# Decode attention with gated feed-forward: scores moved to TensorE, values to VectorE, larger tiles in one ring

## The chip, the cores and the metric

The kernel runs on one core of a Trainium2 chip. A core has a matrix engine (TensorE, PE in the profile, with its weight loads PEld), a vector engine (VectorE, DVE), a scalar engine (ScalarE, ACT), GpSimd (POOL) and SyncE (SP), whose queue issues the transfers here. Each engine takes its own instructions in order and waits on semaphores for the others. Sixteen DMA engines move data from the main memory (HBM) into the on-chip memory (SBUF, 128 partitions); TensorE writes its results to PSUM. The metric is the device time of one execution in microseconds (us), the median of several runs.

## What is computed

For two sequences of one token each, the output is `g * attention + (1 - g) * feed_forward`, all in float32:

```python
B, Sq, D = 2, 1, 448
H, Sk, Dh = 16, 4096, 256          # Dff = 1792

q = (x @ wq).reshape(B, Sq, H, Dh).transpose(0, 2, 1, 3)
scores = jnp.einsum("bhqd,bhkd->bhqk", q, k_cache) * (Dh ** -0.5)
p = softmax(scores)
o = jnp.einsum("bhqk,bhkd->bhqd", p, v_cache)
a = o.transpose(0, 2, 1, 3).reshape(B, Sq, H * Dh) @ wo

b = relu(x @ w1) @ w2
g = sigmoid((x * gate_w).sum(-1, keepdims=True))
return g * a + (1 - g) * b
```

Keys and values are 32 units (16 heads, 2 sequences) of 4096 x 256 numbers each, 4 MB a unit and cache, 268.4 MB together. The weights are another 21.1 MB. Each number is used once.

## The kernel before

A unit `u` is one head `h` and one sequence `b`. Its 4096 keys come as two tiles `k_sb` of 2 MB (128 partitions, 16 keys of 256 numbers in each, a row of 16,384 bytes), its values as two tiles `v_sb` of the same form. `load_cache` (L77) issues all of them from SP. There are four slots for key tiles and five for value tiles. A third ring, `wpool`, has two slots for `w_sb`: one tile (L57) holds the columns of `wq` and the rows of `wo` for two heads, 1.8 MB. The weights `w1` and `w2` take key slots (L202, L233).

- `make_q` (L107): TensorE multiplies x, spread over all partitions, by a head's `wq`, so that the query stands on every partition.
- `score` (L126): VectorE multiplies one key per partition by the query and sums over the 256 numbers, one instruction a key, 32 a unit. Each writes one of four parts of `junk`, which nobody reads, and its sum into `s_sb`.
- `softmax` (L131 to L146): maximum per partition on VectorE, a transpose on TensorE, the maximum over the partitions, its broadcast through TensorE, exponentials on ScalarE, and the sum through TensorE again.
- `attend` (L156): TensorE multiplies the probabilities by the values, 32 matmuls a unit with 256 moving columns, in four column groups that share the array. The trace counts two passes for a float32 matmul.
- `finish` (L170 to L179, `spread` at L163): the head's output is normalised, turned, and multiplied by `wo` into `acc`. The `w_sb` tile is free for its next load only after that.
- `hidden` (L211 to L224) and `mlp_out` (L163): the feed-forward part. Its first half runs beside unit 4; `w2` is the last load, in four pieces.

The order is the program's own. The loop over units loads the keys of unit u+1 and the values of unit u, then scores unit u+1, then attends unit u. All loads stand in SP's queue in that order, so a load that waits for its slot holds up every load behind it. The lines `load_w(h // 2 + 1)` at `u % 4 == 1` put the `w_sb` loads into this queue.

Of the kernel before, what the change touches and what calls it, by code (L numbers as in the profile page):

```python
# [8 lines left out]
F32 = mybir.dt.float32  # L9
# [3 lines left out]

G = 4
KB, VB = 4, 5
NK = 4
# [3 lines left out]
def tile_gated_mix_decode(ctx: ExitStack, tc: tile.TileContext, xg, k_cache, v_cache, wqo, w1, w2, out):  # L20
    nc = tc.nc
    P = 128
    B, H, S, DH = k_cache.shape
    KC = xg.shape[1]
    NF, D = w2.shape[1], w2.shape[2]
    KF = KC - 1
    HP = P // 2
    DG = D // G
    FG = NF * P // G
    NJ = S // P  # L30
    R = P // G
# [18 lines left out]
    w_t, k_t, v_t = {}, {}, {}
    QW = KF * DH

    def load_w(hp):
        w_t[hp] = wpool.tile([P, wqo.shape[2]], F32, name="w_sb")
        nc.sync.dma_start(w_t[hp], wqo[hp])  # L57

    def wq_rows(h, c):
        hp, i = divmod(h, 2)  # L60
        if c < KF:
            return slice(0, P), w_t[hp][:, i * QW + c * DH:i * QW + (c + 1) * DH]
        rows = slice(i * HP, (i + 1) * HP)
        return rows, w_t[hp][rows, 2 * QW:2 * QW + DH]

    def wo_rows(h, t):
        hp, i = divmod(h, 2)
        at = 2 * QW + DH + (2 * i + t) * D
        return w_t[hp][:, at:at + D]

    def load_cache(pool, dst, src, u, c, name, cuts=(0, CH)):
        h, b = divmod(u, B)
        if cuts[0] == 0:
            dst[u, c] = pool.tile([P, CH, DH], F32, name=name)
        view = src[b, h, c * P * CH:(c + 1) * P * CH, :].rearrange("(p j) d -> p j d", p=P)
        for lo, hi in zip(cuts, cuts[1:]):
            nc.sync.dma_start(dst[u, c][:, lo:hi, :], view[:, lo:hi, :])  # L77

    def load_k(u, c):
        load_cache(kpool, k_t, k_cache, u, c, "k_sb")  # L80

    def load_v(u, c, cuts=(0, CH)):
        load_cache(vpool, v_t, v_cache, u, c, "v_sb", cuts)

    load_w(0)
    nc.sync.dma_start(xg_sb, xg)
    for c in range(NCH):
        load_k(0, c)

    ident = const.tile([P, P], F32, name="ident")  # L90
    make_identity(nc, ident)
    ones = const.tile([P, P], F32, name="ones")
    nc.vector.memset(ones, 1.0)

    xb = const.tile([P, KC, B, P], F32, name="xb")
    for b in range(B):
        nc.vector.tensor_scalar(xb[:, :, b, :], xg_sb[:, :, b:b + 1].to_broadcast([P, KC, P]), SCALE, None,  # L97
                                op0=ALU.mult)

    q_t = {}  # L100

    def make_q(h):
        pq = ps_q.tile([P, B, DH], F32, name="pq")
        for b in range(B):
            for c in range(KC):
                rows, w = wq_rows(h, c)
                nc.tensor.matmul(pq[:, b, :], xb[rows, c, b, :], w, start=(c == 0), stop=(c == KC - 1))  # L107
        q_t[h] = work.tile([P, B, DH], F32, name="q_sb")
        nc.scalar.activation(q_t[h], pq, AF.Copy)  # L109

    xr = const.tile([P, KC, P], F32, name="xr")
    for g in range(G):
        nc.vector.tensor_copy(xr[:, :, g * R:(g + 1) * R].rearrange("p c (b r) -> p c b r", b=B),
                              xg_sb[:, :, :B, None].to_broadcast([P, KC, B, R // B]))


    s_t, p_t, l_t, o_t = {}, {}, {}, {}
    junk = const.tile([P, NK, DH], F32, name="junk")

    def score(u, c):  # L120
        h, b = divmod(u, B)
        if c == 0:
            s_t[u] = work.tile([P, NJ], F32, name="s_sb", bufs=3)
        for j in range(CH):
            jj = c * CH + j
            nc.vector.scalar_tensor_tensor(junk[:, j % NK, :], k_t[u, c][:, j, :], 1.0, q_t[h][:, b, :],  # L126
                                           op0=ALU.mult, op1=ALU.mult, accum_out=s_t[u][:, jj:jj + 1])

    def softmax(u):
        mp = work.tile([P, 1], F32, name="mp")  # L130
        nc.vector.reduce_max(mp, s_t[u], axis=AX.X)  # L131
        mt = ps_s.tile([P, 512], F32, name="small")
        nc.tensor.transpose(mt[:1, :P], mp, ident)  # L133
        nm = work.tile([1, 1], F32, name="nm")
        nc.vector.tensor_reduce(nm, mt[:1, :P], axis=AX.X, op=ALU.max, negate=True)  # L135
        mb = ps_s.tile([P, 512], F32, name="small")
        nc.tensor.matmul(mb[:, :1], ones[:1, :], nm, start=True, stop=True)  # L137
        nmb = work.tile([P, 1], F32, name="nmb")
        nc.scalar.activation(nmb, mb[:, :1], AF.Copy)  # L139
        p_t[u] = work.tile([P, NJ], F32, name="p_sb", bufs=3)  # L140
        lp = work.tile([P, 1], F32, name="lp")
        nc.scalar.activation(p_t[u], s_t[u], AF.Exp, bias=nmb, accum_out=lp)  # L142
        lb = ps_s.tile([P, 512], F32, name="small")
        nc.tensor.matmul(lb[:, :1], ones, lp, start=True, stop=True)  # L144
        l_t[u] = work.tile([P, 1], F32, name="li", bufs=3)
        nc.vector.reciprocal(l_t[u], lb[:, :1])  # L146

    def attend(u, c):  # L150
        if c == 0:
            o_t[u] = ps_o.tile([P, DH], F32, name="po")
        for j in range(CH):
            jj = c * CH + j
            g = jj % G
            nc.tensor.matmul(o_t[u][g * R:(g + 1) * R, :], p_t[u][:, jj:jj + 1].to_broadcast([P, R]),  # L156
                             v_t[u, c][:, j, :], start=(jj < G), stop=(jj >= NJ - G))

    acc = ps_a.tile([P, DG], F32, name="acc")

    def spread(dst, rows, w, start, stop):
        for g in range(G):
            nc.tensor.matmul(dst[g * R:(g + 1) * R, :], rows, w[:, g * DG:(g + 1) * DG], start=start, stop=stop)  # L163

    ot_ps = {}

    def finish(u):
        h, b = divmod(u, B)
        osb = work.tile([P, DH], F32, name="osb")
        nc.scalar.activation(osb, o_t[u], AF.Copy, scale=1.0 / R)  # L170
        yield
# [159 lines left out]
```

## Time and profile before

| | |
|---|---|
| median of 3 runs | 700.44 us (700.41 to 700.64) |
| the profiled execution's own time | 700.32 us |
| its span, first to last instruction | 698.5 us |
| mean granted TensorE clock | 0.697 |
| data moved | 290.11 MB, 415 GB/s over the span |
| transfers of 2,048 KB for keys, for values | 64, 64 |

A page of the profile gives busy time by engine, the span in 40 equal slices with the DMA rate in each, the DMA queues, and the chain of work that ended last. Rows of groups read: line, engine, operation, written from read, shapes, count, then busy time and mean ns of one, then the idle time before them and what ended it. Rows of windows give the stretch and its length, then busy time of PE, PEld, DVE, ACT and POOL with counts, the granted TensorE clock, the share of 16 DMA engines that was busy, and GB/s. Rows of the timeline give start, duration, engine, line and operation. Rows of waits give the engine and line that waited, what for, the total, how often, and the longest.

### The profile page before, as it was taken

The numbers are of one execution on the slowest core, as the hardware profiler recorded it, in microseconds if no ns is written. First come the engines' busy times: TensorE is split into PE (matmuls) and PEld (weight loads), VectorE is DVE, ScalarE is ACT, GpSimd is POOL, SyncE is SP. The second block draws the span as 40 slices with busy tenths as digits, with TensorE's granted clock in tenths as the row PEclk, the third lists the DMA queues.
The fourth block names the chain that finished last, engine by engine and source line by source line (L and its number), as shares of the span: only waits on it lengthen the run. The fifth ranks groups of instructions, "written<-read, shape, count | busy, mean of one in ns | idle before, by whom it ended". The sixth has DMA issues, their size and how long they took to land.

```text
span 698.5 us, 8750 instructions
## 1 busy us (share of the span) xinstructions
PE 362.8 (52%) x3007; PEld 200.2 (29%) x3007; DVE 381.7 (55%) x2153; ACT 47.1 (7%) x168; POOL 0.7 (0%) x6
## 2 busy tenths in 40 slices
PE   4183646536572454735636455454635537554347
PEld 3042323213241232413314232232312314232224
DVE  0686563466555566545466365564565555665560
ACT  0110000010000000000000001000000000001000
POOL 0000000000000000000000000000000000000000
PEclk9996766667675575756757557575766767667658
DMA  9999999999999999999999999999999999999994
GB/s 367 430 428 428 423 427 428 423 428 425 427 423 405 427 425 428 380 429 430 426 428 374 431 428 428 427 408 431 425 430 425 384 431 425 428 429 425 428 427 191
DMA packets 20652, 290.11 MB, mean 415 GB/s; under 512 B 2432, under 2 KB 2560, under 8 KB 2816
## 3 DMA queue, kind: packets, MB, share of 16 engines
q1 hardware_dynamic: 20608, 289.56, 98.1%
q8 instruction: 23, 0.38, 0.2%
q14 instruction: 21, 0.17, 0.1%
HBM read 289.54 MB, written 0.00 MB: 415 GB/s over the span
## 4 chain that ended last, share of the span: by engine, by line
DMA 82%; DVE 14%; PE 3%; issue 0%; ACT 0%; SPq 0%; DVEq 0%
DMA k_sb<-in_k_cache 77%; DVE junk L126 13%; DMA k_sb<-in_w 5%; PE pq L107 1%; DMA xg_sb<-in_xg 1%; PE po L156 1%; PE pq L211 0%; PE small L192 0%; PE y L163 0%; DVE xb L97 0%; SPq L77 0%; ACT q_sb L109 0%; PE small L137 0%; DVE mp L131 0%; PE small L144 0%
## 5 line engine op out<-in xcount | busy, mean ns | idle before, releaser
L126 DVE SCALAR_TENSOR_TENSOR junk<-k_sb,q_sb 128x256 f32<-128x256 f32 x1024 | 359.2, 421 | 209.8 <-DMA k_sb<-in_k_cache 201.6
L156 PE MATMUL po<-v_sb,p_sb 128*32 128x256 f32 x2048 | 197.6, 554 | 76.2 <-DMA v_sb<-in_v_cache 76.2
L156 PEld LDWEIGHTS po<-v_sb,p_sb 128*32 128x32 f32 x2048 | 83.5, 150 | 163.1 <-issue 149.1
L133 PE MATMUL small<-ident,mp 128*1 128x128 f32 x32 | 11.8, 369 | 204.4 <-DVE mp L131 204.4
L126 DVE DVE_READ_ACCUMULATOR junk<-k_sb,q_sb 128x1 f32 x1024 | 84.5, 83 | 0.0
L107 PE MATMUL pq<-w_sb,xb 128*128 128x256 f32 (+1 forms) x256 | 80.4, 455 | 0.0
L133 PEld LDWEIGHTS small<-ident,mp 128*1 128x1 f32 x32 | 2.5, 79 | 210.6 <-DVE mp L131 197.7
L107 PEld LDWEIGHTS pq<-w_sb,xb 128*128 128x128 f32 (+1 forms) x256 | 50.4, 218 | 33.2 <-issue 28.0
L146 DVE RECIPROCAL li<-small 128x1 f32<-128x1 f32 x32 | 5.4, 168 | 63.8 <-PE small L144 63.8
L139 ACT ACTIVATE nmb<-small 128x1 f32<-128x1 f32 x32 | 5.5, 171 | 378.9 <-PE small L137 378.9
L144 PE MATMUL small<-lp,ones 128*128 128x1 f32 x64 | 18.5, 359 | 23.9 <-ACT p_sb L142 23.9
L176 PEld LDWEIGHTS ot<-li,osb 128*128 128x128 f32 x128 | 20.6, 228 | 19.0 <-issue 18.1
L137 PE MATMUL small<-nm,ones 1*128 1x1 f32 x64 | 18.4, 354 | 12.0 <-DVE nm L135 12.0
L176 PE MATMUL ot<-li,osb 128*128 128x1 f32 x128 | 23.4, 286 | 0.5 <-ACT osb L170 0.5
L144 PEld LDWEIGHTS small<-lp,ones 128*128 128x128 f32 x64 | 15.8, 306 | 26.6 <-ACT p_sb L142 26.6
L137 PEld LDWEIGHTS small<-nm,ones 1*128 1x128 f32 x64 | 15.7, 303 | 21.2 <-DVE nm L135 20.5
L109 ACT ACTIVATE q_sb<-pq 128x512 f32<-128x512 f32 x16 | 9.6, 597 | 137.9 <-PE pq L107 137.9
L135 DVE TENSOR_REDUCE nm<-small 1x1 f32<-1x128 f32 x32 | 8.9, 278 | 14.9 <-PE small L133 14.9
L170 ACT ACTIVATE osb<-po 128x256 f32<-128x256 f32 x32 | 12.2, 381 | 69.6 <-PE po L156 69.6
L163 PE MATMUL acc<-w_sb,ots 128*32 128x112 f32 x256 | 9.8, 273 | 5.0 <-ACT ots L179 5.0
L142 ACT ACTIVATE p_sb<-s_sb,nmb 128x32 f32<-128x32 f32 x32 | 10.3, 321 | 1.0
L280 DVE SCALAR_TENSOR_TENSOR res<-y,gate,a_sb 128x112 f32<-128x112 f32 x1 | 0.3, 334 | 14.1 <-PE y L163 14.1
(31 smaller groups left out, 44.3 us busy)
## 6 DMA issues: line engine op xcount, KB each, us to landing
k_sb<-in_k_cache SPq DMA_DIRECT2D x64, 2048.0 KB, 34.3
v_sb<-in_v_cache SPq DMA_DIRECT2D x64, 2048.0 KB, 38.8
w_sb<-in_wqo SPq DMA_DIRECT2D x8, 1792.0 KB, 9.1
k_sb<-in_w SPq DMA_DIRECT2D x3, 1568.0 KB, 32.6
k_sb<-in_w SPq DMA_DIRECT2D x1, 896.0 KB, 35.2
k_sb<-in_w SPq DMA_DIRECT2D x1, 448.0 KB, 31.5
k_sb<-in_w SPq DMA_DIRECT2D x1, 224.0 KB, 27.2
xg_sb<-in_xg SPq DMA_DIRECT2D x1, 6.0 KB, 7.2
```

What stands on the lines that cost most here:

```text
L107: nc.tensor.matmul(pq[:, b, :], xb[rows, c, b, :], w, start=(c == 0), stop=(c == KC - 1))
L109: nc.scalar.activation(q_t[h], pq, AF.Copy)
L126: nc.vector.scalar_tensor_tensor(junk[:, j % NK, :], k_t[u, c][:, j, :], 1.0, q_t[h][:, b, :], op0=ALU.mult, op1=ALU.mult, accum_out=s_t[u ...
L133: nc.tensor.transpose(mt[:1, :P], mp, ident)
L135: nc.vector.tensor_reduce(nm, mt[:1, :P], axis=AX.X, op=ALU.max, negate=True)
L137: nc.tensor.matmul(mb[:, :1], ones[:1, :], nm, start=True, stop=True)
L142: nc.scalar.activation(p_t[u], s_t[u], AF.Exp, bias=nmb, accum_out=lp)
L144: nc.tensor.matmul(lb[:, :1], ones, lp, start=True, stop=True)
L156: nc.tensor.matmul(o_t[u][g * R:(g + 1) * R, :], p_t[u][:, jj:jj + 1].to_broadcast([P, R]), v_t[u, c][:, j, :], start=(jj < G), stop=(jj > ...
L163: nc.tensor.matmul(dst[g * R:(g + 1) * R, :], rows, w[:, g * DG:(g + 1) * DG], start=start, stop=stop)
L170: nc.scalar.activation(osb, o_t[u], AF.Copy, scale=1.0 / R)
L176: nc.tensor.matmul(ot[:, t * B + b:t * B + b + 1], osb[:, t::2], l_t[u], start=True, stop=True)
```

## The change

- Keys are laid out with the 256 numbers of a key on partitions (two halves `t` of 128), so that a unit's keys are one tile of 4 MB, 128 rows of 32,768 bytes. Values are laid out with 32 of the 256 columns and one quarter of the positions on a partition, eight rows `j` of 1024 positions each, again one tile of 4 MB.
- All tiles, keys, values and weights, go through one ring of five slots (`ring`, 32 KB a partition and slot), loaded by SP in the program's order. The small `xg` is loaded from ScalarE's queue.
- `scores`: TensorE multiplies the query by the keys, 16 matmuls a unit with 512 moving columns. The four column groups are four quarters of the positions, so that each quarter of the partitions holds the scores of its 1024 positions. Each quarter has its own maximum (`nm`, VectorE, from PSUM) and its own sum (`ls`, with the exponentials on ScalarE).
- `values`: VectorE multiplies the 1024 probabilities by a row of the values and sums, eight instructions a unit. All write the same `junk`, so each waits for the one before.
- `combine`, once for eight heads: scales the quarters to a common maximum, divides by the sum, applies the gate, adds the quarters. `project` multiplies by half of `wo`.
- `make_q` for all heads at the start, from two tiles of `wq`. The first half of `wo` is loaded after unit 16, the rest at the end: `w1`, the other half of `wo`, and `w2` in three pieces.
- `mlp_out` adds the feed-forward part into the same `acc`; the four column groups are added by a matmul with `fold`, and the last two blocks of `w2` go straight to the result.

```diff
-G = 4
-KB, VB = 4, 5
-NK = 4
+G = 4
+R = P // G
+SLOTS = 5
+NB = 2
...
+    ring = ctx.enter_context(tc.tile_pool(name="ring", bufs=SLOTS))
...
+    def load(src, shape, cuts=None):
+        t = ring.tile([P, T * S], F32, name="slot")
...
+        if cuts is None:
+            nc.sync.dma_start(flat, src)
...
-    def score(u, c):
...
-            nc.vector.scalar_tensor_tensor(junk[:, j % NK, :], k_t[u, c][:, j, :], 1.0, q_t[h][:, b, :],
-                                           op0=ALU.mult, op1=ALU.mult, accum_out=s_t[u][:, jj:jj + 1])
...
+    def scores(u, k):
...
+        for c in range(SG // CW):
+            for t in range(T):
+                for g in range(G):
+                    lo = t * S + g * SG + c * CW
+                    nc.tensor.matmul(ps[g * R:(g + 1) * R, c * CW:(c + 1) * CW],
+                                     qt[i][:, s, t, hp, b:b + 1].to_broadcast([P, R]), k[:, lo:lo + CW],
+                                     start=(t == 0), stop=(t == T - 1))
+        nc.vector.tensor_reduce(nm[i][:, at:at + 1], ps, axis=AX.X, op=ALU.max, negate=True)
+        p = work.tile([P, SG], F32, name="p")
+        nc.scalar.activation(p, ps, AF.Exp, bias=nm[i][:, at:at + 1], accum_out=ls[i][:, at:at + 1])
+        return p
...
-            nc.tensor.matmul(o_t[u][g * R:(g + 1) * R, :], p_t[u][:, jj:jj + 1].to_broadcast([P, R]),
-                             v_t[u, c][:, j, :], start=(jj < G), stop=(jj >= NJ - G))
...
+    def values(u, p, v):
+        i, at = place(u)
+        for j in range(J):
+            nc.vector.scalar_tensor_tensor(junk, v[:, j * SG:(j + 1) * SG], 1.0, p, op0=ALU.mult, op1=ALU.mult,
+                                           accum_out=ov[i][:, at, j:j + 1])
...
+    for u in range(U):
+        if u + 1 < U:
+            if u == UB:
+                late["wo"] = load(wo[0], (P, wo.shape[2]))
+            fetch(u + 1)
+        else:
+            late["w1"] = load(w1, (P, w1.shape[1]))
+            late["wo1"] = load(wo[1], (P, wo.shape[2]))
+            late["w2"] = load(w2.rearrange("p k d -> p (k d)"), (P, NF * D),
+                              (0, 6 * D, (NF - TAIL) * D, NF * D))
+        p = scores(u, ks[u])
+        values(u, p, vs[u])
+        if u == UB + 1:
+            project(combine(0), late["wo"], True)
+    hr = hidden(late["w1"])
+    project(combine(1), late["wo1"], False)
+    mlp_out(hr, late["w2"])
```

Where the instructions stand now. First SP's queue, before, around the load of `w1` and the next load of `w_sb`:

```order
L77 DMA k_sb_498<-in_k_cache 128x4096
L77 DMA v_sb_500<-in_v_cache 128x4096
L202 DMA k_sb_590<-in_w1 128x3136
L202 DMA k_sb_592<-in_w1 128x3136
L77 DMA k_sb_594<-in_k_cache 128x4096
L77 DMA v_sb_596<-in_v_cache 128x4096
L77 DMA k_sb_598<-in_k_cache 128x4096
L77 DMA v_sb_600<-in_v_cache 128x4096
L57 DMA w_sb_739<-in_wqo 128x3584
L77 DMA k_sb_741<-in_k_cache 128x4096
```

SP's queue of the changed kernel, around the only weights that are loaded in mid-run (`slot_670` holds the values of unit 16):

```order
L55 DMA slot_668<-in_kt 128x8192
L55 DMA slot_670<-in_vt 128x8192
L55 DMA slot_700<-in_wo 128x7168
L55 DMA slot_702<-in_kt 128x8192
L55 DMA slot_704<-in_vt 128x8192
L55 DMA slot_734<-in_kt 128x8192
L55 DMA slot_736<-in_vt 128x8192
```

A load is now 4 MB and there are half as many; weights stand among them in one place instead of nine.

VectorE before, from the end of the first unit's scores (`s_sb_128`) to the second's (`s_sb_197`):

```order
L131 TENSOR_REDUCE mp_161<-s_sb_128 128x1
L135 TENSOR_REDUCE nm_165<-small_163 1x1
L146 RECIPROCAL li_176<-small_174 128x1
L126 SCALAR_TENSOR_TENSOR junk_107,s_sb_197<-k_sb_178,q_sb_126 128x256 x16
L126 SCALAR_TENSOR_TENSOR junk_107,s_sb_197<-k_sb_182,q_sb_126 128x256 x16
L131 TENSOR_REDUCE mp_247<-s_sb_197 128x1
```

VectorE of the changed kernel, the first three units (`ps` are scores in PSUM, `p` probabilities, `slot` the values, `ov0` their sums):

```order
L156 TENSOR_REDUCE nm0_100<-ps_192 128x1
L164 SCALAR_TENSOR_TENSOR junk_106,ov0_104<-slot_136,p_210 128x1024 x8
L156 TENSOR_REDUCE nm0_100<-ps_224 128x1
L164 SCALAR_TENSOR_TENSOR junk_106,ov0_104<-slot_190,p_242 128x1024 x8
L156 TENSOR_REDUCE nm0_100<-ps_256 128x1
```

A unit's 32 products of 256 became eight of 1024, over values instead of keys, and of the small steps between units one reduction is left.

TensorE at the end, before, from the last unit's second half on:

```order
L156 MATMUL po<-v_sb,p_sb 32x256 x16
L176 MATMUL ot<-li,osb 128x1 x2
L163 MATMUL acc<-w_sb,ots 32x112 x8
L163 MATMUL y<-k_sb,h_sb 32x112 x56
```

TensorE of the changed kernel, from the scores of the second group's later units to the end (`pw` is a PSUM tile that many steps share):

```order
L153 MATMUL ps<-slot,qt_99 32x512 x224
L218 MATMUL pw<-slot,xr 32x448 x16
L224 MATMUL pw<-ident,hs 128x128 x3
L226 MATMUL pw<-ident,hs 64x128 x2
L173 MATMUL pw<-ident,nm_101 16x128
L174 MATMUL pw<-ident,ls_103 16x128
L189 MATMUL pw<-ident,wb 128x16
L195 MATMUL pw<-os,sel 32x32 x4
L207 MATMUL acc<-slot,ot 32x448 x16
L242 MATMUL acc<-slot,hr 32x448 x12
L248 MATMUL pw<-a_sb,fold 32x112 x4
L252 MATMUL pw<-slot,hr 32x112 x8
```

The first half of the feed-forward part, the combination of eight heads and their projection now stand behind the last scores, ahead of the multiplication by `w2`.

More of the change, by code (lines that the diff above doesn't have):

```diff
@@ L66, in wo_rows @@
[L66 to L77, printed above, removed]
@@ L129, in softmax @@
[L129 to L146, printed above, removed]
@@ L186, in tile_gated_mix_decode @@
-    gate = const.tile([P, 2], F32, name="gate")
-    def make_gate():
-        pg = ps_s.tile([P, 512], F32, name="small")
-        for c in range(KC):
-            rows = slice(0, P if c < KF else HP)
-            nc.tensor.matmul(pg[:, :1], xr[rows, c, :], xg_sb[rows, c, B:], start=(c == 0), stop=(c == KC - 1))
-        nc.scalar.activation(gate[:, 0:1], pg[:, :1], AF.Sigmoid)
-        nc.vector.tensor_scalar(gate[:, 1:2], gate[:, 0:1], -1.0, 1.0, op0=ALU.mult, op1=ALU.add)
-    ff = {}
-    def load_w1():
-        for i in range(2):
-            ff["w1", i] = kpool.tile([P, w1.shape[2]], F32, name="k_sb")
-            nc.sync.dma_start(ff["w1", i], w1[i])
@@ L206, in hidden, with project @@
+    def project(ot, w, first):
+        for k in range(HH * J):
+            hh, j = divmod(k, J)
+            g = k % G
+            nc.tensor.matmul(acc[g * R:(g + 1) * R, :], flat(ot[:, hh, j]), w[:, k * D:(k + 1) * D],
+                             start=(first and k < G), stop=False)
+    def hidden(w):
+        ph = psum()
+        half = w1.shape[1] // 2
         for c in range(KC):
@@ L274, in tile_gated_mix_decode, with mlp_out @@
-    for _ in finish(U - 1):
-        pass
-    a_sb = const.tile([P, DG], F32, name="a_sb")
-    nc.scalar.activation(a_sb, acc, AF.Copy, scale=gate[:, 0:1])
-    mlp_out()
-    res = const.tile([P, DG], F32, name="res")
-    nc.vector.scalar_tensor_tensor(res, ff["y"], gate[:, 1:2], a_sb, op0=ALU.mult, op1=ALU.add)
-    nc.sync.dma_start(out, res[::R // B, :])
+        return hr
+    TAIL = 2
+    def mlp_out(hr, w):
+        n = NF - TAIL
+        for k in range(n):
+            g = k % G
+            nc.tensor.matmul(acc[g * R:(g + 1) * R, :], hr[:, k, :], w[:, k * D:(k + 1) * D], start=False,
+                             stop=(k >= n - G))
+        a_sb = const.tile([P, D], F32, name="a_sb")
+        nc.vector.tensor_copy(a_sb, acc)
+        z = psum()
+        for g in range(G):
+            nc.tensor.matmul(z[g * R:(g + 1) * R, :DG], flat(fold), a_sb[:, g * DG:(g + 1) * DG], start=True,
+                             stop=False)
+        for k in range(n, NF):
+            for g in range(G):
+                nc.tensor.matmul(z[g * R:(g + 1) * R, :DG], hr[:, k, :], w[:, k * D + g * DG:k * D + (g + 1) * DG],
+                                 start=False, stop=(k == NF - 1))
+        res = const.tile([P, DG], F32, name="res")
+        nc.vector.tensor_copy(res, z[:, :DG])
+        nc.sync.dma_start(out, res[::RB, :])
```

304 lines of the change are left out of this document (151 added, 153 removed).

## The prediction

> **What bounds the kernel now.** I read the page's shares first, then the rate by slice, then the chain that ended last.
>
> ```profile
> span 698.5 us, 8750 instructions
> PE 362.8 (52%) x3007; PEld 200.2 (29%) x3007; DVE 381.7 (55%) x2153; ACT 47.1 (7%) x168; POOL 0.7 (0%) x6
> GB/s 367 430 428 428 423 427 428 423 428 425 427 423 405 427 425 428 380 429 430 426 428 374 431 428 428 427 408 431 425 430 425 384 431 425 428 429 425 428 427 191
> q1 hardware_dynamic: 20608, 289.56, 98.1%
> q8 instruction: 23, 0.38, 0.2%
> q14 instruction: 21, 0.17, 0.1%
> DMA 82%; DVE 14%; PE 3%; issue 0%; ACT 0%; SPq 0%; DVEq 0%
> ```
>
> No engine is busy over 55%, and the DMA queue that brings the inputs fills 98.1% of 16 engines' span: the transfers set the time. So what counts is their rate, the places where they pause, and what follows the last byte. The rate, in stretches without a pause (the last two columns are the DMA share and GB/s):
>
> ```profile
> 20.00:30.00 10.00, 0.00 (x0) 0.00 (x0) 9.55 (x55) 0.42 (x1) 0.00 (x0) 1.00 1.02 435
> 120.00:130.00 10.00, 4.58 (x52) 2.29 (x47) 5.76 (x35) 0.22 (x1) 0.00 (x0) 0.67 1.00 416
> 304.00:372.00 68.00, 35.08 (x274) 18.73 (x267) 39.26 (x222) 3.62 (x14) 0.00 (x0) 0.60 1.01 429
> 570.00:680.00 110.00, 54.66 (x463) 30.03 (x452) 65.46 (x369) 6.50 (x25) 0.00 (x0) 0.66 1.01 427
> ```
>
> Full is 427 GB/s; single windows of 10 us scatter from 416 to 435. Five pauses stand out, each at a load of `w_sb`, whose slot the PE frees late:
>
> ```profile
> 200.00:220.00 20.00, 12.80 (x116) 7.21 (x109) 11.24 (x65) 1.68 (x6) 0.00 (x0) 0.76 0.98 404
> 290.00:300.00 10.00, 4.29 (x57) 2.21 (x55) 5.81 (x33) 1.10 (x3) 0.00 (x0) 0.87 0.88 341
> 370.00:390.00 20.00, 13.60 (x113) 7.64 (x105) 10.24 (x59) 1.68 (x6) 0.00 (x0) 0.77 0.94 382
> 460.00:470.00 10.00, 2.51 (x41) 1.30 (x33) 5.81 (x33) 0.25 (x2) 0.00 (x0) 0.73 0.98 397
> 540.00:560.00 20.00, 11.80 (x105) 6.69 (x103) 10.24 (x59) 1.68 (x6) 0.00 (x0) 0.75 0.95 389
> SPq L57 <- PE acc L163: 170.7, 6, 30.5
> 294.30 0.33 SPq L57 DMA_DIRECT2D w_sb<-in_wqo  x1
> ```
>
> SP stood up to 30.5 us in front of a `w_sb` load with all later loads behind it. Against 427 the windows lost 20·(1−404/427) = 1.1, then 2.0, 2.1, 0.7 and 1.8: **7.7 us**. The end:
>
> ```profile
> 688.00:690.00 2.00, 1.89 (x33) 0.90 (x32) 0.00 (x0) 0.04 (x1) 0.00 (x0) 1.00 0.50 194
> 690.00:692.00 2.00, 1.29 (x32) 1.21 (x36) 0.00 (x0) 0.57 (x3) 0.00 (x0) 1.00 0.06 24
> 692.00:694.50 2.50, 2.25 (x88) 1.76 (x76) 0.00 (x0) 0.35 (x1) 0.00 (x0) 1.00 0.09 32
> 694.53 0.93 PE L163 MATMUL y<-k_sb,h_sb 128*32 128x112 f32 x24 [0.16 <-DMA k_sb<-in_w]
> 695.62 0.33 DVE L280 SCALAR_TENSOR_TENSOR res<-y,gate,a_sb 128x112 f32<-128x112 f32 x1 [14.05 <-PE y L163]
> 695.98 0.71 SPq L281 DMA_DIRECT2D out<-res  x1
> ```
>
> A DMA share of 0.06 is one engine of sixteen. So from about 690 to 694.6 one engine finishes alone: **4.6 us** of lag. From the trace's single records, a tile's sixteen landings lie 1.3 us apart at the start and 6.5 at the end; the spread grows by about 1 us after an instruction packet (q8, 16 KB) and shrinks by about 2 in each pause. I read this as one thing: an engine that also fetches instructions falls behind, and the pauses only let it catch up. Its total excess is 7.7 + 4.6 = 12.3 us. After the last landing (695.03) come 3.5 us.
>
> **The change, part by part.** Sums are made against the span of the profiled execution, 698.5; its time was 700.32, 1.82 more, and the median of the runs is 700.44.
>
> *Longer rows.* Bytes are the same. The trace's packet records, by size:
>
> ```
> bytes   packets   median ns
>  1792       128          74
>  3584       128         140
> 12544       384         472
> 14336      1024         538
> 16384     16407         612
> ```
>
> The line through 3,584 and 16,384 is 7.8 ns + 0.03688 ns per byte. A row of 32,768 would take 1,216 ns where two took 1,224, so 64 tiles × 8 rows per engine × 8 ns = 4.1, with 64 fewer completion writes of 9 ns 0.6, and the weights' longer rows 0.3: **−5.0 us**. Bounds: 0 if a row is cut in two; at most −6.2 by the windows (289.54 MB at 427 is 678.1 us, at 435 665.6; half of that difference if all of it is cost per row). I take −5.0, which lies by the packet rows.
>
> *No `w_sb` ring.* All weights but one go through the same five slots as keys and values. The two `wq` tiles lie ahead of everything; `wo[0]` sits between tile 16's values and tile 17's keys, and its slot is taken again only four tiles later, some 39 us of transfers after it, with the head outputs ready about 20 us after values 17 land. Nothing on SP should wait for a late engine: **−7.7 us**. If that cover is gone, a stall there costs some 2 us once.
>
> *Engine work per unit* must hide under its 8.39 MB, 19.5 us:
>
> ```profile
> L126 DVE SCALAR_TENSOR_TENSOR junk<-k_sb,q_sb 128x256 f32<-128x256 f32 x1024 | 359.2, 421 | 209.8 <-DMA k_sb<-in_k_cache 201.6 <-ACT q_sb L109 8.3
> 58.16 5.63 DVE junk L126 x32
> L131 DVE TENSOR_REDUCE mp<-s_sb 128x1 f32<-128x32 f32 x32 | 6.0, 186 | 1.1
> L135 DVE TENSOR_REDUCE nm<-small 1x1 f32<-1x128 f32 x32 | 8.9, 278 | 14.9 <-PE small L133 14.9
> L109 ACT ACTIVATE q_sb<-pq 128x512 f32<-128x512 f32 x16 | 9.6, 597 | 137.9 <-PE pq L107 137.9
> L170 ACT ACTIVATE osb<-po 128x256 f32<-128x256 f32 x32 | 12.2, 381 | 69.6 <-PE po L156 69.6
> 641.17 3.64 PE L156 MATMUL po<-v_sb,p_sb 128*32 128x256 f32 x32
> 641.20:644.80 3.60, 3.60 (x33) 1.35 (x32) 2.45 (x14) 0.00 (x0) 0.00 (x0) 0.50 1.03 437
> 647.45 1.93 PE L156 MATMUL po<-v_sb,p_sb 128*32 128x256 f32 x32 [2.64 <-DMA v_sb<-in_v_cache]
> 647.50:649.30 1.80, 1.80 (x32) 1.04 (x32) 0.64 (x4) 0.00 (x0) 0.00 (x0) 1.00 1.02 437
> ```
>
> DVE: the sixteen products of a 256-long tile follow each other at 0.35 us. Between the reductions, 96 more elements cost 92 ns, about 0.96 ns each, as loosely do ScalarE's (0.84). So a product over 1,024 is 421 + 768·1.04 = 1,220 ns, and with the read of its sum and the wait on the one `junk` tile 1.26; eight are 10.1. The maximum over 1,024 is about 1.2. That is 11.3 of 19.5 us; if products scaled with no gain from length (4 × 0.35 = 1.4) it would still be 12.4. PE: the same 32 passes as one value tile, twice as long, 7.3 us at clock 0.50 and 3.9 at 1.00. ScalarE: 1.2. A tile's slot is thus free at most about 12 us after it lands, where four other tiles (39 us) are queued. All hidden: **0**.
>
> *Fewer instructions.* A matmul that is one row in the program is two passes with a weight load each. PE falls from 6,014 instructions to some 2,630 (the order holds 663 matmuls, ten of them transposes of one pass), DVE from 2,153 to some 590. Instruction packets should fall to 0.44 of before, and the excess of the late engine from 12.3 to 5.4 us. No pause lets it catch up, so all of it stands at the end: **+0.8** on the 4.6. Bounds: −4.6 if nothing is late, +7.7 if the excess has nothing to do with instructions.
>
> *The end.* Behind the last values now follow `w1`, `wo[1]`, `w2`: 10.1 MB, 23.5 us. From the landing V of the last values: `w1` is there at V+7.5. Its 32 passes of 448 columns scale to 6.4 us at clock 0.50 and 3.4 at 1.00; PE has been idle, and the burst at 641 shows that 3.6 us of work run wholly at 0.50. With 5 us at half: V+13.2. Relu, five transposes (DVE free of values since V+10.2), two transposes of the statistics: V+15.3. Then eight dependent small steps on DVE, ScalarE and PE, each 0.2 to 0.5 by the small rows: V+18.5. `project` and `mlp_out` are 56 passes, 5 us at half clock for 25 and 3.3 for the rest: V+26.8, though the last bytes came at V+23.6. Copy of the sum 0.65, `fold` 0.5, last two blocks 0.75 (0.93 for 24 passes now), result 0.35, output 2.55 as now: **8.2 us** behind the last landing against 3.5, **+4.7**. Bounds: +1.5 if all of `project` runs at full clock and only the fold stays, +7.5 if PE never leaves half.
>
> The Trainium skill ("TensorE: Matmul & The Clock Gate", Part 1: the HAM clock gate) says that the clock doubles after one busy window of about 3.4 us. The burst at 641, 3.6 us long at 0.50, is barely at odds with it; with 3.4 in the place of 5 the two bursts would be some 1.5 us shorter, and the sum 691.5.
>
> Sum: 698.5 − 5.0 − 7.7 + 0.8 + 4.7 = 691.3; with 1.82 it is 693.1, and 0.1 more for the median: **about 693**.
>
> **Rivals.**
>
> *The end is short* (PE warm, steps overlap): +1.5 in place of +4.7, **690**. For it: at 647 the PE runs at 1.00 soon after a burst. Against: the burst at 641. 0.17.
>
> *Rows are cut, no gain in rate*: 693 + 5.0 = **698**. For it: no row above 16 KB is in this trace. Against: five sizes lie on one line. 0.13.
>
> *One engine is slow by itself.* Then the excess of 12.3 stays and all of it stands at the end: 693 + 6.9 = **700**, no change. For it: the lag is seen directly, its cause is inferred. Against: it grows in steps, not evenly. 0.08.
>
> *Long rows read slower.* Sixteen engines then walk rows that start 32 KB apart in lockstep. The sum has 7.3 us to lose: the break-even is a rate of 289.54 MB / (672.1 + 7.3 us) = 426 GB/s where I forecast 430.8. At 416, the lowest full window, the transfers take 696.0 and the time is **717**, slower. Against it: 12,544, 14,336 and 16,384 fall on one line, so a power of two costs nothing at 16 KB. 0.07.
>
> The Trainium skill ("DMA: Bandwidth & Descriptors", Latency and other measured facts) speaks for this rival: copies between HBM tensors ran at 207 GB/s with a row pitch of 512 KiB, 164 with 2 MiB and 103 with 4 MiB, and it advises a padded pitch or contiguous tiles. It has no rate for 32 KiB, the tiles here are contiguous, and no row of this trace has that pitch.
>
> **How the numbers follow.** The forecast, 693 within some 2.5 us, has 0.55; the rivals have 0.17, 0.13, 0.08 and 0.07. A measurement of this kernel can tell about 0.2% (1.4 us) from no change. Faster: the forecast, the short end, the cut rows and a little of the slow engine, 0.87. Same 0.05, slower 0.08. The range runs from the short end with somewhat less lag, 688, to the slow engine's 699.5; outside lie the slow rows, half of the slow engine's case, and the rare case that both gains run high.
>
> **What would show it.** Right: DMA near 431 GB/s from 20 to 650 us with no pause at `wo`; DVE about 11.3 us of each 19.5; instruction packets near 10 on q8; a share of 0.06 for some 5 us at the end; 8 us between the last landing of `w2` and the end, half of them PE. Wrong: a steady rate at or below 427 (rows cut or slow), SP waiting for PE or DVE in mid-run, or the output following `w2` within 5 us.

## The result, and the profile after

The changed kernel takes **684.1 us** (median of four runs, 683.6 to 684.3); the kernel before took 700.5 on the same chip (700.4 to 700.6). The ratio is 0.9764, 95% interval 0.9747 to 0.9781. The forecast was 693.0 with a range of 688 to 699.5: the direction was right, the size was not, and the time lies below the range. The profiled execution took 683.6, its span is 681.8.

The page of the changed kernel, with the rows that answer to those of before, and two of its costliest groups:

```profile
span 681.8 us, 3558 instructions
PE 215.8 (32%) x1311; PEld 57.6 (8%) x1311; DVE 361.1 (53%) x569; ACT 44.4 (7%) x77; POOL 0.7 (0%) x6
GB/s 377 430 433 440 437 433 431 432 433 431 431 432 433 431 429 439 442 434 431 433 430 431 430 430 434 431 433 437 438 431 433 433 432 434 431 433 430 429 434 181
q1 hardware_dynamic: 10384, 289.55, 98.6%
q8 instruction: 10, 0.16, 0.1%
q14 instruction: 7, 0.06, 0.0%
DMA 80%; DVE 12%; PE 6%; issue 1%; SPq 0%; ACT 0%; ACTq 0%; DVEq 0%
L164 DVE SCALAR_TENSOR_TENSOR junk<-slot,p 128x1024 f32<-128x1024 f32 x256 | 313.4, 1224 | 92.1 <-DMA slot<-in_vt 83.0
L156 DVE TENSOR_REDUCE nm<-ps 128x1 f32<-128x1024 f32 x32 | 39.2, 1225 | 196.9 <-PE ps L153 196.9
```

The transfers still set the time. The five dips of before (374 to 408 in the row of GB/s) are gone, and no slice between the first and the last is under 429. VectorE is nearly as busy as before, 361 us for 382, with a quarter of the instructions (569 for 2,153); a product over 1,024 elements takes 1,224 ns and the maximum 1,225, as forecast. Instruction packets fell from 23 to 10 on q8 and from 21 to 7 on q14.

The waits of SP, the queue that issues the loads:

```profile
SPq L55 <- DVE junk L164: 297.2, 29, 12.3
SPq L55 <- PE acc L207: 8.2, 1, 8.2
```

The longest wait is 12.3 us, where 39 us of transfers are queued ahead, and the load that takes the slot of `wo` waits 8.2: nothing runs dry. (SP waiting for VectorE in mid-run was one of the prediction's signs of being wrong; here the sign came and costs nothing.) The chain that ended last, its end (start, duration, what):

```profile
622.67 36.86 DMA slot<-in_w
...
659.57 5.08 PE pw L218 x32
...
664.68 0.70 DVE hs L221
...
670.01 4.80 PE acc L207 x32
674.81 2.31 PE acc L242 x24
...
677.14 0.64 DVE a_sb L245
...
677.92 0.40 PE pw L248 x8
678.32 0.42 PE pw L252 x16
...
678.76 0.28 DVE res L255
```

After `w1` landed (659.53) the end is a chain of TensorE's work with small steps between; `w2` is no longer on it.

From the single records of the traces, the last tile's landings on the sixteen DMA engines, for the kernels of this section and of the experiments (us; "behind" is from the last landing to the end of the span; the spread of the first tiles is 0.7 to 0.9 in the changed kernel and its variants, 1.3 before):

```
kernel                    DVE instr  q8 q14   first    15th    16th  spread  behind
before                         2153  23  21  688.53  690.48  695.02    6.50    3.52
e2, three weight slots         2153  23  21  678.60  684.48  695.57   16.96    3.53
e7, two keys at once           1129  23  13  678.53  684.45  687.22    8.69    3.54
changed                         569  10   7  671.20  674.12  675.43    4.23    6.38
e3, more on TensorE             569  23   7  671.26  676.04  676.19    4.92    7.21
e5, more on VectorE            2069  10  18  671.28  674.21  685.55   14.27    6.39
e1, rows of 16 KB               569  10   8  674.08  676.95  678.29    4.21    7.02
e10, e1 moved by 32 B           569  10   8  679.58  682.74  684.45    4.87    7.00
e14, changed moved by 32 B      569  10   7  674.21  677.60  679.06    4.86    6.06
```

### The profile page after: what moved, and what is told of

It is laid out like the page before. It is cut to its first block, busy times and chain, and to the rows that moved or that the text cites. A ratio compares the mean times of both kernels' runs of the same rounds, so it can differ in the third digit from the quotient of the medians.

```text
span 681.8 us, 3558 instructions
## 1 busy us (share of the span) xinstructions
PE 215.8 (32%) x1311; PEld 57.6 (8%) x1311; DVE 361.1 (53%) x569; ACT 44.4 (7%) x77; POOL 0.7 (0%) x6
## 4 chain that ended last, share of the span: by engine, by line
DMA 80%; DVE 12%; PE 6%; issue 1%; SPq 0%; ACT 0%; ACTq 0%; DVEq 0%
DMA slot<-in_vt 47%; DMA slot<-in_kt 28%; DVE junk L164 12%; DMA slot<-in_w 5%; PE ps L153 4%; PE pw L218 1%; PE acc L207 1%; PE acc L242 0%; SPq L55 0%; DVE hs L221 0%; DVE a_sb L245 0%; PE pw L224 0%; ACT hr L228 0%; DVE ot L199 0%; PE pw L252 0%
## 5 line engine op out<-in xcount | busy, mean ns | idle before, releaser
L164 DVE SCALAR_TENSOR_TENSOR junk<-slot,p 128x1024 f32<-128x1024 f32 x256 | 313.4, 1224 | 92.1 <-DMA slot<-in_vt 83.0
L153 PE MATMUL ps<-slot,qt 128*32 128x512 f32 x1024 | 180.0, 867 | 416.6 <-DMA slot<-in_kt 416.6
L156 DVE TENSOR_REDUCE nm<-ps 128x1 f32<-128x1024 f32 x32 | 39.2, 1225 | 196.9 <-PE ps L153 196.9
L153 PEld LDWEIGHTS ps<-slot,qt 128*32 128x32 f32 x1024 | 45.2, 152 | 550.5 <-issue 532.9
L158 ACT ACTIVATE p<-ps,nm 128x1024 f32<-128x1024 f32 x32 | 35.7, 1114 | 569.7 <-DVE nm L156 569.7
L164 DVE DVE_READ_ACCUMULATOR junk<-slot,p 128x1 f32 x256 | 20.8, 81 | 0.0
L207 PE MATMUL acc<-slot,ot 128*32 128x448 f32 x64 | 10.4, 817 | 1.1 <-DVE ot L199 1.1
L122 PE MATMUL pw<-slot,xr 128*32 128x512 f32 (+1 forms) x64 | 10.5, 794 | 0.0
L218 PE MATMUL pw<-slot,xr 128*32 128x448 f32 (+1 forms) x32 | 5.0, 778 | 11.7 <-DMA slot<-in_w 11.7
L158 ACT ACTIVATION_READ_ACCUMULATOR p<-ps,nm 128x1 f32 x32 | 6.2, 193 | 0.0
L218 PEld LDWEIGHTS pw<-slot,xr 128*32 128x32 f32 (+1 forms) x32 | 1.1, 150 | 15.7 <-DMA slot<-in_w 12.6
```

The lines of the kernel that those rows point to most:

```text
L122: nc.tensor.matmul(pq[g * R:(g + 1) * R, :], flat(xr[r, c]), w[r, at:at + CW], start=(c == 0), stop=(c == KC - 1))
L153: nc.tensor.matmul(ps[g * R:(g + 1) * R, c * CW:(c + 1) * CW], qt[i][:, s, t, hp, b:b + 1].to_broadcast([P, R]), k[:, lo:lo + CW], start=( ...
L156: nc.vector.tensor_reduce(nm[i][:, at:at + 1], ps, axis=AX.X, op=ALU.max, negate=True)
L158: nc.scalar.activation(p, ps, AF.Exp, bias=nm[i][:, at:at + 1], accum_out=ls[i][:, at:at + 1])
L164: nc.vector.scalar_tensor_tensor(junk, v[:, j * SG:(j + 1) * SG], 1.0, p, op0=ALU.mult, op1=ALU.mult, accum_out=ov[i][:, at, j:j + 1])
L207: nc.tensor.matmul(acc[g * R:(g + 1) * R, :], flat(ot[:, hh, j]), w[:, k * D:(k + 1) * D], start=(first and k < G), stop=False)
```

## The experiments

All ratios are to the kernel before on the same chip, with 95% intervals.

### The pauses and the late engine

**e2.** The kernel before with a third slot for `w_sb`, so that no load waits for TensorE:

```diff
-NK = 4
+NK = 2
...
-    wpool = ctx.enter_context(tc.tile_pool(name="wpool", bufs=2))
+    wpool = ctx.enter_context(tc.tile_pool(name="wpool", bufs=3))
```

> The kernel before with a third slot for w_sb, so that its loads no longer wait for the projection of the heads two tiles back (the unused part of junk is halved to make room). Theory of the prediction (one late engine sets the end, and the pauses only let it catch up): the pauses go, the late engine's work stays, so the time stays at 700 within 1.5, and the stretch at the end with a DMA share of about 0.06 grows from 4.6 us to 10 or more. Rival (the pauses cost their time themselves): 7.7 to 11 us less, 690 to 693, with the stretch at the end still about 5 us.

Measured: 700.44 us, ratio 1.0000 (0.9991 to 1.0009). Windows of e2 at two of the five pauses and over the end:

```profile
290.00:300.00 10.00, 4.63 (x59) 2.66 (x57) 5.81 (x33) 1.09 (x3) 0.00 (x0) 0.92 1.01 430
370.00:390.00 20.00, 13.90 (x113) 7.98 (x109) 10.74 (x61) 1.68 (x6) 0.00 (x0) 0.76 1.01 427
...
684.00:688.00 4.00, 4.00 (x48) 1.85 (x40) 0.00 (x0) 0.38 (x1) 0.00 (x0) 0.57 0.06 27
688.00:692.00 4.00, 3.33 (x48) 2.03 (x40) 0.00 (x0) 0.52 (x2) 0.00 (x0) 1.00 0.06 24
```

Where before had 341 and 382 GB/s there are 430 and 427. The first engine is done at 678.6 instead of 688.5, and the time is the same to 0.1%, since one engine (a share of 0.06) goes on alone until 695.57. So five pauses that look like a loss of 7.7 us **cost nothing**: the late engine sets the end, and it was working through them. Its whole lag is 16.96 − 1.28 = 15.7 us.

### Who makes it late

**e3.** The changed kernel with unused TensorE work, 28 matmuls of one column after each of 30 units:

```diff
+        if u < U - 2:
+            idle = psum()
+            for _ in range(28):
+                nc.tensor.matmul(idle[:R, :1], flat(xr[:, 0]), xg_sb[:, 0, B:], start=True, stop=True)
```

> The changed kernel with 28 more one-column matmuls after each of the first 30 units, whose results nothing uses: PE has as many instructions as in the kernel before, and 4 us more work in each 19.4. Theory (the engine that also fetches instructions is the late one): instruction packets on q8 rise from 10 to about 23, the spread of the last landings from 4.2 to 8 or more, the time by 4 to 5, to 688.5. Rival (the lag has another cause): 684, spread 4.2.

Measured: 685.62 us, 0.9784 (0.9771 to 0.9798). TensorE's matmuls rise from 1,311 to 2,991 and q8 from 10 packets to 23, as in the kernel before, and the spread only to 4.92, 1.5 us in the time. The theory falls: it isn't TensorE's instructions. The single records say why they weigh so little. A packet of q8 does put an engine back, but not the same one each time: the packet at 26.0 us widens the spread by 1.4, the one at 55.3 puts a second engine back by 1.3, and the spread next grows by so much at the packets at 248.9 and 471.8, each the eighth after the one before. At the end eight engines land 4.4 to 4.9 us behind the first and the other seven at most 2.8; in the changed kernel one engine is over 3 us behind.

**e5.** The changed kernel with unused VectorE work, 50 memsets of one column after each of 30 units:

```diff
+    idle = const.tile([P, 64], F32, name="idle")
...
+        if u < U - 2:
+            for j in range(50):
+                nc.vector.memset(idle[:, j:j + 1], 0.0)
```

> The changed kernel with 50 one-column memsets on VectorE after each of the first 30 units, of a tile that nothing reads: VectorE has about as many instructions as in the kernel before and stays under 17 of each 19.4 us. New theory (one engine fetches VectorE's instructions, the 8 KB packets of q14, and each costs it about 1 us; PE's fetches go round several engines): q14 rises from 7 to 18 or 19 packets, the spread of the last landings from 4.2 to about 15, the time by 11 to 12, to 695. Rival (the lag follows something else that the change removed): 684 to 685, spread 4 to 5.

Measured: 693.94 us, 0.9906 (0.9893 to 0.9920). The page and the windows of e5:

```profile
PE 218.7 (32%) x1311; PEld 58.2 (8%) x1311; DVE 384.6 (56%) x2069; ACT 44.4 (6%) x77; POOL 0.7 (0%) x6
q8 instruction: 10, 0.16, 0.1%
q14 instruction: 18, 0.15, 0.1%
676.00:680.00 4.00, 1.41 (x17) 0.77 (x16) 1.42 (x8) 1.07 (x4) 0.00 (x0) 1.00 0.05 23
680.00:684.00 4.00, 3.87 (x24) 1.11 (x28) 0.41 (x2) 0.00 (x0) 0.00 (x0) 0.57 0.08 31
```

VectorE is 24 us busier of 692, far from a bound. Eleven more packets on q14 (8 KB of VectorE's instructions each), 10.0 us more spread, 9.8 us more time. From the single records: the packets of q14 in mid-run, and the spread of the tiles around them.

```
q14 packet at   spread of the tiles before -> after
       131.3    1.82 -> 2.79
       169.7    2.73 -> 3.69
       204.5    3.65 -> 4.59
       241.7    4.54 -> 5.45
       281.4    5.40 -> 6.39
       312.5    6.35 -> 7.30
```

Each of these puts one engine back by 0.95 us, though the packet itself takes some 0.31, and nothing gives it back. Fourteen of the sixteen packets from 131 us to the end of the loads stand by such a step; those at 371.6 and 386.4 don't.

**e7.** The other way round: e2 with one VectorE instruction for two keys. What it leaves out is the score of each single key: the two keys of a pair share one score, the sum of theirs, and one probability.

```diff
...
-        for j in range(CH):
-            jj = c * CH + j
-            nc.vector.scalar_tensor_tensor(junk[:, j % NK, :], k_t[u, c][:, j, :], 1.0, q_t[h][:, b, :],
+        for j in range(0, CH, 2):
+            jj = (c * CH + j) // 2
+            nc.vector.scalar_tensor_tensor(junk, k_t[u, c][:, j:j + 2, :], 1.0,
+                                           q_t[h][:, b:b + 1, :].to_broadcast([P, 2, DH]),
...
-            nc.tensor.matmul(o_t[u][g * R:(g + 1) * R, :], p_t[u][:, jj:jj + 1].to_broadcast([P, R]),
+            nc.tensor.matmul(o_t[u][g * R:(g + 1) * R, :], p_t[u][:, jj // 2:jj // 2 + 1].to_broadcast([P, R]),
```

> The kernel before with three slots for w_sb, and VectorE multiplying two keys in one instruction of 512, so that a pair of keys shares the sum of their scores: half as many instructions on VectorE, the same on PE. New theory (the late engine is VectorE's fetch engine, and it alone sets the end of this kernel): q14 falls from 21 to 12 or so, the spread at the end from 17 to 9, the time by 7 to 8, to 693. Rival (the fetches of PE make the lag): 700.

Measured: 692.64 us, 0.9887 (0.9874 to 0.9901), spread 8.69. Half of VectorE's instructions gone, q14 down from 21 packets to 13, VectorE just as busy (379 us for 382), and 7.8 us gone from e2.

### Long rows

**e1.** The changed kernel with each 4 MB tile loaded as two transfers of 16,384 B rows:

```diff
+        if cuts is None and n == T * S:
+            cuts = tuple(i * n // 2 for i in range(3))
```

> The changed kernel with each 4 MB tile of keys or values loaded by two transfers of half rows (16,384 bytes) in place of one of 32,768; all else as it is. Theory (a row has a fixed cost): two rows of 16 KB took 2 x 612 ns in the kernel before, one of 32 KB takes 1,213 in the changed kernel; 64 tiles x 8 rows x 11 ns = 5.6 us and 64 more completion writes 0.6, so 6 us longer, 690. Rival (the rate comes from the missing pauses, not from the rows): 684, no change.

Measured: 686.74 us, 0.9809 (0.9795 to 0.9822): between the two. Rows of 32,768 B are worth 2.6 us here. The packets of 16,384 B took 611 ns, nearly all, where the kernel before had 611 to 622: something other than length differed.

**e6.** e1 with the halves packed one after the other in HBM, so that rows start 16 KB apart as in the kernel before (the host lays out the same numbers in another order, values likewise, and `load` takes the two halves one by one):

```diff
...
-    kt = np.asarray(A_k_cache).reshape(B, H, S, T, P).transpose(1, 0, 4, 3, 2).reshape(U, P, T, S)
+    kt = np.asarray(A_k_cache).reshape(B, H, S, T, P).transpose(1, 0, 3, 4, 2).reshape(U, T, P, S)
...
```

> The half-row kernel of the first call, with the same loads of 16,384-byte rows, but each half of a tile packed in HBM by itself, so that its rows follow each other every 16 KB as in the kernel before, and not every 32 KB. Theory (the layout in HBM makes the packets of the kernel before scatter from 611 to 621 ns): 686.7 + 3.9 = 690.5, packets of 614 to 616 in the mean. Rival (the scatter comes from what the engines of the kernel before do beside the transfers): 686.7, packets of 611.

Measured: 686.79 us, 0.9808 (0.9794 to 0.9821), 611 ns. The distance between rows in HBM isn't it.

### Where rows start in SBUF

The built programs put the first `k_sb` of the kernel before at byte 32,352 of its partition, 96 past a multiple of 256, and the first `slot` of the changed kernel at 29,696, a multiple of 512. An unused tile in front moves all of them; N is 8, 104 or 40 numbers (32, 416, 160 B):

```diff
+    pad = const.tile([P, N], F32, name="pad")
+    nc.gpsimd.memset(pad, 0.0)
```

**e9** (kernel before, 32 B) and **e10** (e1, 32 B):

> The kernel before with one unused tile of 32 B a partition allocated ahead of all others (a memset of it on GpSimd is added work). It moves every tile that the K and V transfers write by 32 B: the first k_sb from byte 32,352 of its partition to 32,384, so from 32 past a multiple of 64 to a multiple of 64. Nothing else differs. Alignment theory (before's 16,384 B packets take 611 to 622 ns with a mean of 614 to 616, those of the changed kernel and of its half-row runs exactly 611 or 1,213, because before's rows land 32 B off): packets all 611 ns, 2 MB tiles 4.86 us apart in place of 4.893, 128 tiles x 0.03 = 3.9 us less: 696.6 us. Rival (the scatter comes from something else, such as the kernel's many VectorE instructions): packets still 611 to 622 and 700.5 us.

> The changed kernel with each 4 MB tile loaded as two transfers of 16,384 B rows (e1), and the same unused tile of 32 B ahead of all others: its slots now start 32 B past a multiple of 64 (29,728 in place of 29,696). Alignment theory: packets scatter over 611 to 622 ns as in the kernel before, 4 MB tiles 9.79 us apart in place of 9.725, 64 x 0.06 = 3.9 us more than e1's 686.7: 690.6 us. Rival (something else): packets of exactly 611 ns and 686.7 us.

Measured: e9 700.31 us, 0.9998 (0.9989 to 1.0007), nothing; e10 693.02, 0.9894 (0.9880 to 0.9907), 6.3 more than e1. By e9 the theory falls as it was put, a multiple of 64; by e10 the start does matter. Left were the larger multiples.

**e12** (kernel before, 416 B) and **e13** (160 B):

> The kernel before with an unused tile of 416 B a partition ahead of all others (a memset of it on GpSimd is added work), so that k_sb, v_sb and w_sb all start at multiples of 512 B of their partition (the first k_sb at 32,768; before at 32,352, in e9 at 32,384). In e9 a multiple of 128 changed nothing; in e10 a shift of 32 B from a multiple of 512 cost 6.3 us and scattered the packets over 613 to 621 ns. Theory (rows are moved fastest where they start at a multiple of 512 B): packets of exactly 611 ns, 2 MB tiles 4.86 us apart in place of 4.893, 4 to 6 us less: 695 us. Rival (the scatter in the kernel before has another cause): packets 611 to 622 and 700.4 us.

> As e12 with an unused tile of 160 B: k_sb, v_sb and w_sb start at odd multiples of 256 B (the first k_sb at 32,512). If a multiple of 256 B is enough: packets of 611 ns and 695 us as e12. If it must be 512: packets 611 to 622 and 700.4 us.

Measured: e12 694.44 us, 0.9911 (0.9898 to 0.9925); e13 694.04, 0.9907 (0.9893 to 0.9920). They gain 6.2 and 6.6 us without any other edit: a multiple of 256 B is what counts.

**e14** (changed kernel, 32 B) and **e15** (e7, 416 B):

> The changed kernel with an unused tile of 32 B ahead of all others, so that its slots start 32 B past a multiple of 512 (29,728 in place of 29,696); rows stay 32,768 B. Theory (the loss goes with the bytes: e1 to e10 lost 0.076 us per 4 MB): packets near 1,219 ns and above, 4.9 to 6.3 us more: 689 us, so that this part of the gain over the kernel before belongs to where the slots happen to start. Rival A (the loss is per row, so half for rows twice as long): 687 us. Rival B (rows of 32,768 B don't lose): 684.1 us.

> e7 (the kernel before with three weight slots and one VectorE instruction for two keys, so that the two share the sum of their scores) with an unused tile of 416 B ahead of all others, so that k_sb, v_sb and w_sb start at multiples of 512 B (the first k_sb at 30,720; in e7 at 30,304, which is 96 past a multiple of 512). Theory (the late engine and the start of the rows add up): e7's 692.6 less 4 to 6 us: 688 us, with nothing of the scores moved to TensorE and rows of 16,384 B. Rival (the late engine hides it): 692.6 us.

Measured: e14 686.90 us, 0.9807 (0.9794 to 0.9821), which is rival A, a loss per row; e15 687.41, 0.9812 (0.9799 to 0.9825), which adds up as the theory said. From the single records of packets (bytes past a multiple of 256; the share of packets at or under 611 ns, or 1,213 for long rows; their mean; and what lies between two tiles in mid-run):

```
kernel             past 256  row bytes  at 611/1213  mean ns   us per tile
before                   96     16384         0.31     615.1   4.894 of 2 MB
e9                      128     16384         0.40     615.1   4.894
e12                       0     16384         0.99     612.2   4.862
e13                       0     16384         0.99     612.4   4.862
e1                        0     16384         1.00     611.4   4.862
e10                      32     16384         0.02     616.1   4.901
changed                   0     32768         1.00    1213.9   9.682 of 4 MB
e14                      32     32768         0.03    1218.8   9.724
```

A row that starts 32 B off the boundary takes 4.7 or 4.9 ns more, whether it has 16 or 32 KB (e10 against e1 616.1 − 611.4, e14 against the changed kernel 1,218.8 − 1,213.9); 96 B off it is 2.9 (before against e12, 615.1 − 612.2). For e14, eight rows an engine and tile make 0.04 us a tile; by the distance between tiles, 9.724 − 9.682, 64 tiles lose 2.7 us, measured 2.8. In e12 and e13 the distance gives 128 × 0.032 = 4.1 of the 6.2 to 6.6; most of the rest shows in mid-run pauses that are about 1.1 shorter and a last spread that is 0.5 to 0.9 narrower. The Trainium skill ("DMA: Bandwidth & Descriptors", How a descriptor splits into AXI transactions) says that a descriptor (here a row) is cut at multiples of 256 B, and that in one which starts off them the first transaction begins at the boundary below and spends time on bytes that aren't used. It says so of reads; here only the written side was moved, and the runs agree with it in the boundary (a start at a multiple of 128 does nothing, at one of 256 it does) and in the price per row.

### The end

**e4** and **e8.** The changed kernel with unused matmuls of 512 columns ahead of `hidden` (40 in e4, 52 in e8) and 9 beside `combine`, so that TensorE doesn't idle:

```diff
+    def warm(n, k):
+        t = ps_s.tile([P, SG], F32, name="ps")
+        for j in range(n):
+            g = j % G
+            nc.tensor.matmul(t[g * R:(g + 1) * R, :CW], k[:, :R], k[:, :CW], start=True, stop=True)
...
+    warm(52, ks[U - 1])
-    project(combine(1), late["wo1"], False)
+    project(combine(1, lambda: warm(9, ks[U - 1])), late["wo1"], False)
```

> The changed kernel with 40 matmuls of 512 columns behind the last scores and 9 beside the last combination, whose results nothing uses, so that PE is busy before w1 lands and before the last projection. Theory (after the last landing the end is a chain on PE, and its first half runs at half clock): hidden falls from 5.0 to 3.5 us, project from 4.8 to 3.5, and the end comes 1.5 us sooner, when the last landing begins to set it, 682.6. Rival (the landing sets it already, or the clock stays at half): 684; if the added work delays hidden, 685 or more.

> As the kernel with added matmuls of the first call, with 52 in place of 40 behind the last scores, so that they end at about 659.4, when w1 lands, and not 2.6 us ahead of it. Theory (the clock had fallen back in those 2.6 us, so hidden still ran at half): hidden falls from 5.0 to 3.5 us, and the end moves by another 0.8, until the landing of w2 sets it: 682.2. Rival (hidden is not on the path, or the added work delays it): 683 or more.

Measured: e4 682.97 us, 0.9749 (0.9736 to 0.9763); e8 682.72, 0.9746 (0.9733 to 0.9759). The chain of e8:

```profile
649.23 11.16 PE ps L175 x104
...
660.38 3.19 PE pw L226 x32
...
669.86 3.21 PE acc L215 x32
673.07 3.15 PE acc L250 x24
```

The 32 passes of `hidden` took 5.08 us after an idle stretch and 3.19 right behind other work, those of `project` 4.80 and 3.21. The granted clock of the changed kernel in these two stretches (0.50 is half):

```profile
659.57:663.00 3.43, 3.43 (x20) 0.99 (x24) 2.69 (x6) 0.00 (x0) 0.00 (x0) 0.50 1.06 460
670.00:673.20 3.20, 3.19 (x20) 0.99 (x24) 0.29 (x1) 0.00 (x0) 0.00 (x0) 0.50 0.64 264
```

By the clock's single records it is half until 663.03 and again from 669.86 to 673.27, so `hidden` ran 3.5 us at half clock and `project` 3.3; in e8 the clock is full through both. (In e4 the 40 matmuls ended 2.6 us too early: the clock fell to half 1.1 us after `hidden` had begun, for 3.4 us, and `hidden` still took 4.98.) The Trainium skill ("TensorE: Matmul & The Clock Gate", Part 1: the HAM clock gate) has the clock double after a busy stretch of about 3.4 us: the trace agrees. Only 1.4 us of the 3.5 that the two parts gained (1.89 + 1.59) reach the time, 0.9 between the profiled executions: `hidden` starts 0.8 later, behind the added matmuls, the small steps up to `project` take 0.9 longer with the 9 among them, and `mlp_out` (L250) takes 0.8 longer, since it now waits for a piece of `w2`.

**e11.** e8 with `w2` cut after ten blocks in place of six:

```diff
-                              (0, 6 * D, (NF - TAIL) * D, NF * D))
+                              (0, 10 * D, (NF - TAIL) * D, NF * D))
```

> The changed kernel with 52 and 9 unused matmuls that keep TensorE busy (e8) and with w2 cut after ten blocks in place of six, so that the second piece holds two blocks of w2 and not six. In e8 mlp_out waited for the second piece (landed 674.45) and then did six blocks (24 matmul instructions). Theory (the end is the matmul work behind the last landings): the second piece's work falls to two blocks, end some 0.9 us earlier: 681.8 us. Rival (the first, larger piece lands no earlier than the second did, since all the pieces share one late engine): the same 682.7 us.

Measured: 682.58 us, 0.9745 (0.9732 to 0.9758): the rival. From e11's chain:

```profile
642.54 31.29 DMA slot<-in_w
...
673.87 2.51 PE acc L250 x24
```

All of `mlp_out` waits for the larger piece. e8 and e11 (682.4 to 683.0 in nine runs) beat the changed kernel (683.6 to 684.3 in four) by 1.4 to 1.5 us, at the price of work for nothing.

## Why the prediction was too slow

Its sum and what the runs gave, as steps in the time. Between the kernel before and e10 lies all of the change but longer rows and a lucky start of the slots; e10 to e14 are the longer rows, e14 to the changed kernel is the start of the slots. (These ran on several chips; the kernel before took 700.4 to 700.6 on each.)

```
step                                         forecast   measured
pauses, late engine, end                         -2.2       -7.5   before 700.5 -> e10 693.0
longer rows                                      -5.0       -6.1   e10 693.0 -> e14 686.9
where the slots start                              --       -2.8   e14 686.9 -> changed 684.1
sum                                              -7.2      -16.4
```

*What bounds the kernel.* Right: DMA before and after, every engine's work per unit hidden, and one engine that lands last. That the pauses only let it catch up was right too, and stronger than the text made it: with all pauses gone the time doesn't move (e2).

*No `w_sb` ring, −7.7, and fewer instructions, 12.3 falls to 5.4.* The step that failed. No load waits for long, as forecast, but the price of the pauses and the lag were read apart and added, 7.7 + 4.6 = 12.3, where the lag alone, unhelped, is 15.7 (e2). And the excess was put down to q8, TensorE's instructions, and scaled by their 0.44. It is q14, VectorE's: 0.95 us a packet on one engine (e5), where q8's are shared out over eight (e3). VectorE's instructions fell to 0.26, and the lag from 15.7 to 4.23 − 0.78 = 3.4 us, not to 5.4; the stretch with one engine alone, put at some 5 us, is 1.3 (674.12 to 675.43). The trace of before had q14 with 21 packets next to q8 with 23; their times against the steps of the spread would have told the two apart: in its single records the spread grows by some 0.96 around the q14 packets at 183.2, 227.6 and 577.0, and by nothing around the q8 packets at 163.7, 317.3 and 591.6.

*Longer rows, −5.0.* Right for rows that start off the boundary, as before's did: by the distance between tiles 2 × 4.901 − 9.724 = 0.078 us, over 64 tiles 5.0; the last landing came 5.4 earlier and the end followed 0.9 closer (e10 to e14). With rows on the boundary, length is worth half as much, 2 × 4.862 − 9.682 = 0.042 us a tile, 2.7 in all, measured 2.6 (e1).

*Where the slots start, not in the sum.* Nothing in the text speaks of it. The scatter from 611 to 622 ns was in the records of before, and it was worth 6.2 to 6.6 us there (e12, e13). A change of layout happened to move the tiles onto the boundary: some 2.8 of the 16.4 us came from it by luck, and more (6.3, e10 against e1) would have come from it had the rows stayed short.

*The end, +4.7 (8.2 us behind the last landing).* Mis-sized: 6.4 behind, +2.9. `hidden` was put at 5.7 and took 5.08; the small steps up to `project` took 5.4, put at 5.3; `project` and `mlp_out` were put at 8.3 and took 4.80 + 2.31. TensorE stood at half clock for 3.5 us of `hidden` and 3.3 of `project`, where the sum had 5 twice.

*Rivals.* Rows are cut: no, one packet of 32,768 B takes 1,213 ns. Long rows read slower: no, the rate rose. One engine slow by itself: no (e5, e7). The short end: half true, 6.4 between its 5.0 and 8.2.

*Two steps of the working.* A product over 1,024 was put at 421 + 768 × 1.04, though the rows beside it give 0.96 ns an element; the measured 1,224 makes it 1.05, so the 1.04 was the better one. The forecast rate of 430.8 GB/s goes with 672.1 us of transfers, where 678.1 − 5.0 is 673.1; the sum of the time doesn't use it, only the rival of slow rows does.

*What stays open.* Before to e10 should gain 15.7 − 4.1 = 11.6 from the lag and lose 3.5 at the end, 8.1, where the spans of the two profiled executions differ by 7.1. The missing 1.0 stands in the landings: the first engine of e10 is done 0.98 after that of e2 (679.58, 678.60), and rows that start 32 B off the boundary put 128 tiles 128 × (4.901 − 4.894) = 0.9 us later than rows 96 B off. Why 32 B costs more than 96, why an 8 KB packet puts its engine back by 0.95 us, and why most of VectorE's packets fall on one engine while TensorE's go round, was not tried.

## What to carry to other kernels

Where transfers fill the span, look at the sixteen engines' landings one by one: a pause in mid-run is free if one engine is late anyway, and the lag went with the number of VectorE's instructions, so one instruction over 1,024 elements beats four over 256 even if VectorE is half idle. Look at where the tiles start in their partition before and after any edit of sizes: 32 B were worth 2.8 to 6.3 us of 690. Packets of one size that scatter by 11 ns in 611 are a reason to ask why before costing anything by their median.

## What the runs showed of the hardware

- A packet of VectorE's instructions (q14, 8 KB) puts one of sixteen DMA engines back by some 0.95 us, and these delays add up on one engine (e5, fourteen of sixteen packets in mid-run). TensorE's packets (q8, 16 KB) go round eight engines, by their landings, so that 13 more widen the last spread by 0.7 in all (e3).
- A row written 32 B off a multiple of 256 B of its partition takes 4.7 ns more with 16 KB and 4.9 with 32 KB (e10, e14), one 96 B off 2.9 (before against e12). TensorE's instruction packets among rows 32 B off take 1,071 ns in the median (e10), and 942 among rows on the boundary (e1).
- Rows that start 32 KB apart in HBM are read at full rate: 1,213 ns, 27.0 GB/s an engine, against 611 ns and 26.8 for 16 KB.
- After an idle stretch TensorE's work began with 3.3 to 3.5 us at half clock (0.50 granted), and unused matmuls right ahead of the work took that away (e8).
